# Fourier mixing beside attention: sequence matrices first, by two levels of seven products

## The chip, the cores and the metric

The kernel runs on one core of a Trainium2 chip. The metric is the device time of one execution in microseconds (us). TensorE (PE in the profile) multiplies matrices into PSUM; VectorE (DVE), ScalarE (ACT) and GpSimd (POOL) work elementwise; SyncE (SP) issues nearly all transfers. The kernel before takes 2942.41 us (median of three runs, 2941.58 to 2943.34).

## The reference

Two independent sublayers on a sequence of 2048 rows and 1024 features, in fp32, written side by side:

```python
qkv = (x @ wqkv)...; p = softmax(q @ k.T * 32 ** -0.5); a = (p @ v) @ wo    # 32 heads of 32
re = einsum("bsd,ed->bse", x, dft_hid_re); im = einsum("bsd,ed->bse", x, dft_hid_im)
b = einsum("ts,bse->bte", dft_seq_re, re) - einsum("ts,bse->bte", dft_seq_im, im)
return concatenate([a, b], axis=-1)
```

The change touches only the second one. Its result is y = Cr x Wr - Ci x Wi (with W transposed), where the sequence matrices C are 2048 x 2048 and the feature matrices W are 1024 x 1024. The product may be taken from either side: first x W and then C (x W), or first C x and then (C x) W.

## The kernel before, in words

**Dense products.** Each fp32 operand is split into a high half (a rounded copy, "cast") and a low half (operand minus high half), and each product of 128x128 by 128x512 takes three matmuls: high·high, low·high, high·low (`group`, line 404 issues them). The operand that is loaded as weights is called a stationary piece (`piece`: 128 x 4 x 128, ring tiles `h` and `l`), the other one moving (`moving`: 128x512, tiles `slot`). `fetch` loads a term into `raw`, a second one into `g`, and adds or subtracts them (line 469); `halves` makes the high half on DVE (line 491), or on ACT where the flag `spare` is set (line 489), and the low half on POOL or DVE (line 494).

**Seven products.** Each large product is cut in halves in all three directions and done with seven half-size products instead of eight (Winograd's form; `ORDER` = 1, 2, 5, 6, 7, 3, 4). The factors are sums of quarters of the operands, made by `fetch`; the products are added into the four result quarters by `gather`, which reads PSUM on DVE (lines 950 to 967) and combines on POOL or DVE (lines 979 to 992). Sums needed twice are stored in DRAM (`s1_d`, `t1_d`, `s2_d`, `t2_d`).

**Fourier part.** `dense1` multiplies x (`in_xb`) with the two feature matrices (`in_wd`) by one level of seven, 8 row blocks by 2 matrices by 4 chunks by 3 matmuls for each of the seven, into `ab_d`. `dense2` then does the sequence matrices (`in_ct`, stationary) on `ab_d` (moving), again one level for each of the two matrices, 8 groups of 24 matmuls for each of 14 products, and adds the two results through `y_d`.

**Attention.** `qkv` makes queries, keys and values with the same dense scheme. For every head, `scores` computes 32 blocks of 128 x 1024 scores (line 1278), their maxima on DVE (line 1284) and exponentials with sums on ACT (line 1287). `transposed` computes the transposed scores in 64 blocks of 128x512 (line 1400), takes the exponential on ACT (line 1404), and multiplies with the values in three blocks per head, "P·V" (line 1419). `project` multiplies the heads' outputs with `wo`, 672 matmuls; its tiles take the room of attention's, so its loads wait for all heads (`behind`).

**The order of the work.** All engines' orders are written out ahead by a planner (class `Plan`, lines 57 to 245) that keeps a clock with fixed costs for each operation. Streams S (scores), T (transposed scores) and V (P·V) belong to attention; the dense matmuls stand in one list, `fills`, in the order qkv, dense1, dense2, project. The main loop at the end of the kernel function starts the next fill if no attention step is ready, or if

```python
nf / (FILL - RES) <= done / ATT
```

where nf counts fills started, done the TensorE cost of attention so far, RES is 400, and ATT the whole cost of attention. On the other engines the ready operation of lowest rank goes first: PSUM reads and maxima come ahead of casts, these ahead of sums. `choose` starts nothing on POOL while DVE runs an operation marked `two` (sums, low halves, casts), and nothing marked `two` on DVE while POOL runs. Rings of few buffers (6 `raw`, 3 `g`, 4 `h`, 4 `l`, 4 `e`) limit how far the vector work runs ahead of the matmuls.

Of the kernel before, what the change touches and what calls it, by code (L numbers as in the profile page):

```python
# [16 lines left out]
P = 128  # L17
# [203 lines left out]
def kernel(  # L221
# [26 lines left out]
    ab_d = [[[dram.tile([P, NB], F32, name=f"ab_d{m}_{e}_{k}") for k in range(NS)] for e in range(2)] for m in range(2)]  # L248

    s1_d = [[dram.tile([P, 4, P], F32, name=f"s1_d{x}_{i}") for i in range(8)] for x in (5, 6)]  # L250
    t1_d = [[dram.tile([P, NB], F32, name=f"t1_d{x}_{n}") for n in range(8)] for x in (5, 6)]
# [5 lines left out]
    u3_d = [[dram.tile([P, NB], F32, name=f"u3_d{i}_{m}") for m in range(2)] for i in range(8)]  # L257
    s2_d = [[[dram.tile([P, 4, P], F32, name=f"s2_d{x}_{i}_{k}") for k in range(4)] for i in range(8)] for x in (5, 6)]
    t2_d = [[[dram.tile([P, NB], F32, name=f"t2_d{x}_{m}_{k}") for k in range(8)] for m in range(2)] for x in (5, 6)]
    y_d = [[dram.tile([P, NB], F32, name=f"y_d{i}_{e}") for e in range(2)] for i in range(NS)]  # L260
# [101 lines left out]
    FILL = 3 * (7 * 24 * 4 + 7 * 16 * 4 + 7 * 8 * 16 + 2 * 8 * 4)  # L362
# [251 lines left out]
    def qkv():  # L614
# [216 lines left out]
        def qk_group(x, W, b, n, order=None):  # L831
# [3 lines left out]
            if p == 1 and n == 0:  # L835
                if early:
                    X[2 * b], X[2 * b + 1] = acc(b)
                else:
# [3 lines left out]
                  gather(p, 2 * b + n, qk_result(b + 8 * h[0], 2 * h[1] + n, early) if h else None, early, None if b % 2 else SCALE), order)  # L842

# [7 lines left out]
        for x, (p, blocks, v) in enumerate(STEPS[:10]):  # L851
            spare[0] = x < 5
# [77 lines left out]

    def gather(what, X, Y, u3, to, wrote, part=None, split=False):

# [13 lines left out]
        def finish(ps, last):  # L946
# [63 lines left out]
            if what in (2, 3):  # L1010
                return put(X.at, [X.users], X.last, ALU.add, to, wrote, part)
            if Y is None:
                return put(lambda: got["c"], [cusers], cload, ALU.subtract, to, wrote, part)
            return put(Y.at, [Y.users], Y.last, ALU.subtract, to, wrote, part)
# [3 lines left out]
    ab_st = [[[[] for _ in range(NS)] for _ in range(2)] for _ in range(2)]  # L1018

    def dense1():  # L1020
        s1, t1 = ({5: [[] for _ in range(8)], 6: [[] for _ in range(8)]} for _ in range(2))
        u3 = [[[], []] for _ in range(8)]

        def a_terms(p, i):
            q = lambda r, k: xb[8 * r + i, :, 4 * k : 4 * k + 4, :]
            return {
                1: [(1, q(0, 0), [])], 2: [(1, q(0, 1), [])], 4: [(1, q(1, 1), [])],
# [17 lines left out]
        def load_b(x, n):  # L1045
            p = ORDER[x]
            B[x][n] = moving((8 * x + n) % 12, b_terms(p, n), (t1_d[p - 5][n], t1[p][n]) if p in (5, 6) else None)

# [542 lines left out]
```

## Time and profile before

| what | value |
|---|---|
| median of three runs | 2942.41 us |
| span of the profiled execution | 2940.5 us |
| matmuls in it | 14920, of them 6720 fills, 8 to warm up, 4096 for scores, 4096 P·V |
| DMA | 562.78 MB, mean 191 GB/s |
| dense1 | loads of its operands from 605.0 us, last store of its result 1460.4 us |
| dense2 | loads of the sequence matrices from 1371.2 to 2753.3 us |
| last P·V block ends | about 2760.5 us |

The profiled execution is one of its own; the time of a run contains some 2 us outside the span from the first to the last instruction. In tables of stretches each row gives start, end and length, then for each engine the busy us and the instructions in brackets, the granted clock as a share, the DMA engines' busy share and GB/s. In groups by line, the numbers behind the first bar are busy us in total and mean ns of one operation, and behind the second the idle time just before them with what ended it. In the order of time, each row has start, length, engine, line and operation, and in square brackets idle time before it.

### The profile page before, as it was taken

What the parts mean: (1) busy time and instruction counts of PE and PEld (TensorE: products, weight loads), DVE (VectorE), ACT (ScalarE), POOL (GpSimd) and SP (SyncE); (2) the same over time, 40 slices, a digit from 0 to 9 for tenths busy, and PEclk for the clock granted to TensorE, in tenths of its full rate; (3) what the DMA queues carried; (4) which work ended last, traced back from release to release, by engine and by line L of the source; (5) the groups of instructions that cost most, each with busy time, mean ns of one, the idle gap of its engine ahead of it and who ended that gap; (6) DMA issues with size and microseconds to landing.
All of it is one profiled execution on the core that took longest, in us unless ns stands there. A gap on an engine that the chain in (4) does not pass through costs nothing.

```text
span 2940.5 us, 45511 instructions
## 1 busy us (share of the span) xinstructions
PE 2934.3 (100%) x14920; PEld 2146.0 (73%) x14920; DVE 2328.2 (79%) x3196; ACT 2278.3 (77%) x4317; POOL 833.3 (28%) x650
## 2 busy tenths in 40 slices
PE   9999999999999999999999999999999999999999
PEld 8887777777777767777777777777777777677787
DVE  7679888788877987777777898888777888887585
ACT  5347888888888888888888888888888888887431
POOL 2324335132212332241111332333112333343042
PEclk9999999999999999999999999999999999999999
DMA  9965668676525653664425775554334677555663
GB/s 372 348 229 194 195 191 292 194 251 225 191 93 164 226 189 111 205 206 147 150 84 161 237 224 189 171 167 151 110 110 139 220 238 222 168 178 176 211 209 118
DMA packets 378455, 562.78 MB, mean 191 GB/s; under 512 B 111183, under 2 KB 111439, under 8 KB 378095
## 3 DMA queue, kind: packets, MB, share of 16 engines
q1 hardware_dynamic: 378076, 559.75, 58.8%
q8 instruction: 120, 1.97, 0.3%
q14 instruction: 115, 0.93, 0.1%
q10 hardware_dynamic: 144, 0.13, 0.0%
HBM read 385.65 MB, written 174.08 MB: 190 GB/s over the span
## 4 chain that ended last, share of the span: by engine, by line
PE 98%; DMA 1%; DVE 1%; ACT 0%; issue 0%; POOL 0%; SPq 0%; DVEq 0%; POOLq 0%; ACTq 0%
PE pd L404 44%; PE psT L1400 16%; PE psS L1278 16%; PE pd L1419 15%; PE psT L404 7%; DVE negm L1284 0%; DMA raw<-in_xb 0%; DMA g<-in_ct 0%; DMA raw<-ab_d 0%; ACT psS L1287 0%; DMA g<-in_xb 0%; DMA slot<-in_xw 0%; DVE l L494 0%; POOL raw L469 0%; DVE raw L469 0%
## 5 line engine op out<-in xcount | busy, mean ns | idle before, releaser
L1404 ACT ACTIVATE pt<-psT 128x512 f32<-128x512 f32 x2048 | 1193.8, 671 | 347.3 <-PE psT L1400 345.5
L1284 DVE TENSOR_REDUCE negm<-psS 128x1 f32<-128x1024 f32 x1024 | 1241.2, 1220 | 211.5 <-PE psS L1278 204.4
L1287 ACT ACTIVATE psS<-psS,negm 128x1024 f32<-128x1024 f32 x1024 | 1188.9, 1161 | 70.9 <-DVE negm L1284 66.8
L404 PE MATMUL pd<-slot,h 128*128 128x512 f32 x3400 | 1155.7, 389 | 0.0
L1400 PE MATMUL psT<-qs,ks 128*128 128x512 f32 x2048 | 802.3, 395 | 0.0
L404 PEld LDWEIGHTS pd<-slot,h 128*128 128x128 f32 x3400 | 638.3, 188 | 132.6
L404 PE MATMUL pd<-slot,l 128*128 128x512 f32 x1700 | 661.3, 389 | 0.0
L1400 PEld LDWEIGHTS psT<-qs,ks 128*128 128x128 f32 x2048 | 381.4, 188 | 157.3 <-issue 63.7
L1278 PE MATMUL psS<-ks,qs 128*128 128x512 f32 x1552 | 472.1, 390 | 0.7 <-ACT psS L1287 0.6
L1419 PE MATMUL pd<-pt,vt 128*32 128x512 f32 x4096 | 459.3, 594 | 0.0
L494 POOL TENSOR_TENSOR l<-raw,h 128x512 fp32r<-128x512 f32 x143 | 184.7, 1292 | 707.8 <-PE psT L1400 366.5
L404 PEld LDWEIGHTS pd<-slot,l 128*128 128x128 f32 x1700 | 319.1, 188 | 67.3 <-issue 0.8
L494 POOL TENSOR_TENSOR slot<-raw,slot 128x512 fp32r<-128x512 f32 x162 | 208.4, 1291 | 535.5 <-DVE slot L491 197.6
L469 POOL TENSOR_TENSOR raw<-raw,g 128x512 f32<-128x512 f32 x186 | 241.9, 1306 | 397.4 <-DMA raw<-t_d 48.9
L1278 PEld LDWEIGHTS psS<-ks,qs 128*128 128x128 f32 x1552 | 290.7, 188 | 62.2 <-ACT psS L1287 3.3
L1419 PEld LDWEIGHTS pd<-pt,vt 128*32 128x32 f32 x4096 | 123.3, 110 | 282.6 <-issue 265.7
L1287 ACT ACTIVATION_READ_ACCUMULATOR psS<-psS,negm 128x1 f32 x1024 | 285.9, 279 | 0.0
L404 PE MATMUL pd<-slot,slot 128*128 128x512 f32 x768 | 191.9, 389 | 0.0
L1432 DVE TENSOR_TENSOR ot<-ot,pd 128x512 f32<-128x512 f32 x64 | 44.0, 687 | 155.1 <-PE pd L1419 154.9
L404 PEld LDWEIGHTS pd<-slot,slot 128*128 128x128 f32 x768 | 144.2, 188 | 30.0
L491 DVE CAST h<-raw 128x512 fp32r<-128x512 f32 x321 | 147.5, 461 | 17.4 <-PE pd L404 14.2
L1278 PE MATMUL psS<-ks,qx 128*128 128x512 f32 x496 | 149.1, 391 | 0.0
(130 smaller groups left out, 1858.4 us busy)
## 6 DMA issues: line engine op xcount, KB each, us to landing
raw<-in_ct SPq DMA_DIRECT2D x192, 256.0 KB
qk_d<-e SPq DMA_DIRECT2D x52, 512.0 KB
qs<-qk_d SPq DMA_DIRECT2D x128, 192.0 KB
ks<-qk_d SPq DMA_DIRECT2D x128, 192.0 KB
raw<-ab_d SPq DMA_DIRECT2D x96, 256.0 KB
g<-in_ct SPq DMA_DIRECT2D x96, 256.0 KB
c<-u_d SPq DMA_DIRECT2D x88, 256.0 KB
s_d<-raw SPq DMA_DIRECT2D x80, 256.0 KB
```

The source lines that it names most:

```text
L404: nc.tensor.matmul(box["ps"], a[1]((a[0].hi, a[0].lo)[u]()), b[1]((b[0].hi, b[0].lo)[v]()), start=k == 0, stop=k == n - 1)
L469: (nc.gpsimd if e == "POOL" else nc.vector).tensor_tensor(out=dest(), in0=dest() if a is None else a.get(), in1=other["q"] if "q" in other ...
L491: nc.vector.tensor_copy(hi(), raw())
L494: (nc.gpsimd if e == "POOL" else nc.vector).tensor_tensor(out=lo(), in0=raw(), in1=f(hi()), op=ALU.subtract)
L1278: nc.tensor.matmul(p[:, i * NB : i * NB + NB], (QX[0] if own else QS[h % 2])[:, qt * P : qt * P + P], KS[h % 2][:, c * 1024 + i * NB : c * ...
L1284: nc.vector.tensor_reduce(out=ST["negm"][:, c, qt : qt + 1], in_=box["p"], axis=AX.X, op=ALU.max, negate=True)
L1287: nc.scalar.activation(box["p"], box["p"], AF.Exp, bias=ST["negm"][:, c, qt : qt + 1], accum_out=ST["sums"][:, c, qt : qt + 1])
L1400: nc.tensor.matmul(box["p"], KS[h % 2][:, t * P : t * P + P], QS[h % 2][:, j * NB : j * NB + NB], start=True, stop=True)
L1404: nc.scalar.activation(box["t"], box["p"], AF.Exp)
L1419: nc.tensor.matmul(po["p"][j * DH : j * DH + DH, :], VT[h][:, k, :], box["t"], start=(k == t0), stop=(k == t), tile_position=(0, j * DH),)
L1432: nc.vector.tensor_tensor(out=po["o"], in0=po["o"], in1=po["p"], op=ALU.add)
```

## The change

`dense1` now multiplies the sequence matrices first, and with two levels of seven: each of the two matrices (r = 0 cosine, r = 1 sine) takes 49 products (pp outer, p inner), each of 2 groups of 12 matmuls. x is stationary (`xb`), the sequence matrix moves (`ct`). A quarter of it, or a sum of two quarters, is held in 16 resident tiles `R` in fp32 for one outer product; the inner products' moving operands are made from `R` in place. The stationary pieces are stored when r = 0 makes them (`ha_d`) and loaded back for r = 1 (`again`). `gather2` adds the inner products in PSUM reads and two accumulators, then the outer ones through `xo_d` and `yo_d`, into `g_d`. `dense2` then does the feature matrices with one level of seven, both matrices in one sum, so `y_d` and its sums go.

`aside`, called in the steps 5 to 7 of `qkv` once after each group, makes the first 30 entries of the list `todo_a` ahead: the 28 stationary pieces of the outer products 1 and 2 and two sums of outer product 5. `spare` stays set after the early steps, so ACT may take casts in all of the Fourier part and of `qkv`. FILL follows the new count of matmuls. Nothing is changed in attention and projection.

```diff
-    FILL = 3 * (7 * 24 * 4 + 7 * 16 * 4 + 7 * 8 * 16 + 2 * 8 * 4)
+    FILL = 3 * (7 * 24 * 4 + 2 * 49 * 2 * 4 + 7 * 8 * 8 + 2 * 8 * 4)
...
+            if 5 <= x < 8:
+                aside((12, 13, 14))
...
         for x, (p, blocks, v) in enumerate(STEPS[:10]):
-            spare[0] = x < 5
+            spare[0] = True
...
+        def outer(y, e, users):
+            if pp == 1:
+                x_at[1][:] = [store(x_at[0], y, e, users)]
+            elif pp == 5:
+                y_at[1][:] = [store(y_at[0], y, e, users)]
+                o = combine(cx[0], cx[0], y, ALU.add, [e, cx[2]], [users, cx[1]])
+                x_at[1][:] = [store(x_at[0], cx[0], o, cx[1])]
+            elif pp == 4:
+                o = combine(y, cy[0], y, ALU.subtract, [e, cy[2]], [users, cy[1]])
+                wrote.append(store(to, y, o, users))
+            else:
+                o = combine(y, cx[0], y, ALU.add, [e, cx[2]], [users, cx[1]])
...
+    def a_piece(pp, p, i):
+        s = lambda x: (si_d[0][pp][x - 5][i], si.setdefault((pp, x, i), []))
+        terms = a_terms(pp, p, i)
+        a = piece(terms, s(p) if p in (5, 6) else None)
+        rank = seq()
+        kept_a[pp, p, i] = [op("SP", ISSUE, lambda k=k, t=t: nc.sync.dma_start(ha_d[pp][p][i][:, k * NB : k * NB + NB], ...), [made], [u], rank, 256)
+                            for k, (t, made, u) in enumerate(zip((a.hi, a.lo), a.made, a.users.lists))]
+        return a
...
+        def b_outer(r, pp, k, n, kk):
+            terms = {
+                1: [(1, *q(0, 0))], 2: [(1, *q(1, 0))], 3: [(1, *q(1, 1))],
+                5: [(1, *q(0, 1)), (-1, *q(0, 0))], 6: [(1, *q(1, 1)), (-1, *t(5))],
+                7: [(1, *q(1, 1)), (-1, *q(0, 1))], 4: [(1, *t(6)), (-1, *q(1, 0))],
+            }[pp]
+            fetch([P, NB], terms, t(pp) if pp in (5, 6) else None, R[j])
...
+        def load_b(x, kk):
+            terms, keep = {
+                1: ([(1, r(0, 0))], None), 2: ([(1, r(1, 0))], None), 3: ([(1, r(1, 1))], None),
+                5: ([(1, r(0, 1)), (-1, r(0, 0))], r(0, 0)), 6: ([(1, r(1, 1)), (-1, r(0, 0))], r(0, 0)),
+                7: ([(1, r(1, 1)), (-1, r(0, 1))], r(0, 1)), 4: ([(1, r(0, 0)), (-1, r(1, 0))], r(1, 0)),
+            }[p]
+            M[x, kk] = moving((4 * x + kk) % 10, terms, None, keep)
...
+        for x, (r, pp, p) in enumerate(steps):
...
+            for i in range(2):
+                a = again(pp, p, i) if (pp, p, i) in kept_a else a_piece(pp, p, i)
...
+                group(((chunk(a, c), (M[x, c], whole)) for c in range(4)), 4,
+                      gather2(pp, p, X[i], Y[i] if p not in (1, 2) else None, (xo_d[r][pos], xo[r][pos]), (yo_d[r][pos], yo[r][pos]), to, wrote))
```

353 lines of the change are left out of this document (249 added, 104 removed).

## The prediction

> **What bounds the kernel now.** I read the page's first two parts first, then the same stretches for all engines and for single lines, and last the instructions in order of time around one P·V block.
>
> ```profile
> span 2940.5 us, 45511 instructions
> PE 2934.3 (100%) x14920; PEld 2146.0 (73%) x14920; DVE 2328.2 (79%) x3196; ACT 2278.3 (77%) x4317; POOL 833.3 (28%) x650
> ...
> PE   9999999999999999999999999999999999999999
> ```
>
> TensorE is never idle, so taking matmuls away looks worth their time. The stretches show why that reading is too short. All engines first; the cuts lie where attention starts (200), where the matmuls of qkv end (772) and where attention ends (2762):
>
> ```profile
> 200.00:772.00 572.00, 572.00 (x2937) 415.25 (x2936) 480.48 (x658) 478.53 (x911) 195.71 (x153) 1.00 0.68 219
> 772.00:1376.00 604.00, 603.66 (x3137) 431.93 (x3139) 476.16 (x635) 515.17 (x985) 152.51 (x119) 1.00 0.53 168
> 1376.00:2000.00 624.00, 623.77 (x3237) 448.57 (x3230) 504.66 (x687) 531.83 (x1019) 163.01 (x127) 1.00 0.55 172
> 2000.00:2600.00 600.00, 599.88 (x3120) 428.82 (x3119) 486.38 (x660) 510.54 (x979) 167.27 (x130) 1.00 0.54 168
> ```
>
> Now the dense matmuls alone (line 404, the "fills"):
>
> ```profile
> 0.00:200.00 200.00, 190.53 (x831) 155.82 (x831) 1.00 0.91 333
> 200.00:772.00 572.00, 340.94 (x1183) 221.81 (x1182) 1.00 0.68 219
> 772.00:1376.00 604.00, 348.09 (x1187) 222.73 (x1187) 1.00 0.53 168
> 1376.00:2000.00 624.00, 357.22 (x1227) 230.44 (x1228) 1.00 0.55 172
> 2762.00:2940.50 178.50, 174.63 (x771) 144.25 (x769) 1.00 0.55 195
> ```
>
> and the transposed scores of attention (line 1400):
>
> ```profile
> 200.00:772.00 572.00, 168.64 (x432) 80.38 (x432) 1.00 0.68 219
> 772.00:1376.00 604.00, 190.58 (x487) 90.42 (x486) 1.00 0.53 168
> 1376.00:2000.00 624.00, 199.25 (x508) 94.72 (x508) 1.00 0.55 172
> 2000.00:2600.00 600.00, 189.69 (x484) 90.15 (x484) 1.00 0.54 168
> ```
>
> Attention moves at one steady pace, 0.81 of these scores per us, whichever Fourier stage lies beside it. The fills take what is left: 1187 in 604 us, 1.96 per us. The order of the program says the same: a fill goes ahead of attention that is ready only where nf / (FILL - RES) <= done / ATT. FILL - RES is 6240 - 400 = 5840. At 1376 us 831 + 1183 + 1187 = 3201 fills are gone, 0.55 of it, and of attention 432 (200 to 772) + 487 of 2048 transposed scores, 0.45. So fills are ahead and attention has the right of way. What sets attention's pace is ScalarE, 511 of 600 us busy, and the rest is mostly one kind of gap:
>
> ```profile
> L1404 ACT ACTIVATE pt<-psT 128x512 f32<-128x512 f32 x2048 | 1193.8, 671 | 347.3 <-PE psT L1400 345.5
> ```
>
> and in order of time:
>
> ```profile
> 1001.39 4.50 PE L1419 MATMUL pd<-pt,vt 128*32 128x512 f32 x40
> ...
> 1006.35 0.60 ACT L1404 ACTIVATE pt<-psT 128x512 f32<-128x512 f32 x1 [2.33 <-PE psT L1400]
> ```
>
> For the 4.50 us of a P·V block TensorE makes no scores and ScalarE runs dry for 2.33 us. There are three such blocks in each of 32 heads, and fills are in none of them. **So there are two bounds at once: TensorE as a sum, and the chain of attention through ScalarE, which ends at 2762 us and which fewer fills don't shorten.** Behind it 771 fills stand, 672 of them the output projection (7·8·4·3), so only 99 are Fourier fills that come late.
>
> **The change part by part.** Every operation is on a 128x512 tile; the counts are read off the loops.
>
> Matmuls. Before: feature stage 7·8·2·12 = 1344, sequence stage 14·8·24 = 2688. After: sequence matrices 2·49·2·12 = 2352, feature matrices 7·8·24 = 1344. That is 336 fewer.
>
> ```profile
> 2800.00:2900.00 100.00, 100.00 (x443) 82.79 (x442) 1.00 0.52 175
> ```
>
> A fill costs 100/443 = 0.2257 us, so 75.8 us of TensorE go.
>
> Vector work. "Two-input" are sums and low halves, for POOL or DVE; casts are high halves; "out" reads PSUM and is DVE's.
>
> - Before, both stages: 768 two-input, 448 casts, 256 out, 1056 transfers.
> - After: sequence stage 1070 two-input (580 sums, 490 low halves), 490 casts, 224 out; feature stage 272, 168 and 64. Together 1342, 658, 288, and about 1654 transfers.
>
> The added work is 574 two-input operations and 210 casts, for fewer matmuls, and it is not spread evenly. The first matrix (cos) makes the stationary pieces, the second (sin) loads them back. 28 pieces, those of the first two of seven outer products, are made early by `aside`. So per fill: the first 336 fills about 0.34 two-input and 0.17 casts; the next 840 (outer products five to four of the first matrix) 482/840 = 0.57 and 210/840 = 0.25; the 1176 of the second matrix 442/1176 = 0.38 and 0.17. Today's sequence stage has 0.21 and 0.125. Out is 0.095 throughout. The prices:
>
> ```profile
> L1284 DVE TENSOR_REDUCE negm<-psS 128x1 f32<-128x1024 f32 x1024 | 1241.2, 1220 | 211.5 <-PE psS L1278 204.4
> L491 DVE CAST h<-raw 128x512 fp32r<-128x512 f32 x321 | 147.5, 461 | 17.4 <-PE pd L404 14.2
> L494 DVE TENSOR_TENSOR l<-raw,h 128x512 fp32r<-128x512 f32 x178 | 127.5, 717 | 3.5
> L494 POOL TENSOR_TENSOR l<-raw,h 128x512 fp32r<-128x512 f32 x143 | 184.7, 1292 | 707.8 <-PE psT L1400 366.5
> L967 DVE TENSOR_TENSOR e<-slot,pd 128x512 f32<-128x512 f32 x126 | 85.9, 682 | 40.9 <-PE pd L404 38.1 <-issue 0.8
> L489 ACT ACTIVATE slot<-raw 128x512 fp32r<-128x512 f32 x58 | 35.6, 630 | 82.6 <-PE psT L404 34.8 <-DVE raw L469 15.6 <-DMA raw<-in_wo 15.4
> ```
>
> The plan (`choose`) starts no POOL operation while DVE is in a two-input operation or a cast, and the reverse; maxima and PSUM reads may lie beside POOL. Attention takes 1024 maxima in some 2500 us, 0.41 per us, at 1.22 = 0.50 of DVE, and its small operations about 0.055 (estimate from their groups). In the heavy stretch at r fills per us, with casts on ScalarE in its gaps (0.15 per us; gaps of 347 us in 2500 would hold 0.22), the best split is r = 1.48: two-input 0.85 per us, of which DVE 0.34 · 0.717 = 0.25 and POOL 0.51 · 1.292 = 0.65; casts on DVE 0.22 · 0.461 = 0.10; out 0.14 · 0.682 = 0.10. DVE is then 0.50 + 0.055 + 0.25 + 0.10 + 0.10 = 1.00, and DVE's share of the port plus POOL 0.25 + 0.10 + 0.65 = 1.00. Nothing is left, and the fills want 1.96. No stretch so far shows such packing; the highest is
>
> ```profile
> 200.00:300.00 100.00, 100.00 (x481) 76.74 (x480) 90.14 (x120) 75.91 (x141) 43.24 (x34) 1.00 0.60 188
> 400.00:500.00 100.00, 100.00 (x509) 73.56 (x501) 87.97 (x125) 87.02 (x168) 54.82 (x44) 1.00 0.78 254
> ```
>
> so I take r = 1.40; bounds 1.2 (DVE at 85%) and 1.5. The second matrix needs by the same sum at 1.96 about 0.95 of DVE; I take 1.96, bound 1.8.
>
> ```profile
> 1001.19 1.28 POOL L469 TENSOR_TENSOR raw<-raw,g 128x512 f32<-128x512 f32 x1 [8.56 <-issue]
> ...
> 1001.50 1.22 DVE L1284 TENSOR_REDUCE negm<-psS 128x1 f32<-128x1024 f32 x1 [0.33 <-PE psS L1278]
> ```
>
> Beside a maximum a POOL sum is no longer than alone. The Trainium skill ("SBUF — State Buffer", Who interferes with whom) states this exclusion for the hardware: a DVE operation with two SBUF inputs, or a cast in a two-port mode, and a GpSimd operation that reads SBUF block each other, a reduction does not. These rows agree for the reduction; that the other two block each other no row here can show, as the plan never lets them meet. Were there no exclusion, POOL could run through, the heavy stretch would keep 1.96, and the sum would be that of the first rival.
>
> Transfers, all on SP's queue:
>
> ```profile
> qs<-qk_d SPq DMA_DIRECT2D x128, 192.0 KB
> ks<-qk_d SPq DMA_DIRECT2D x128, 192.0 KB
> ...
> L453 SPq DMA_DIRECT2D raw<-in_ct x192: 327/333/1007, 1371.2 to 2753.3; - x192
> ```
>
> The second sweep has 532 in 1176 fills, 0.45 · 0.262 MB · 1.96 = 232 GB/s, and attention's own about 32 (estimate: these two and five smaller kinds, 2.5 MB per head of 79 us): 264. The issues take 0.9 per us at 0.33, a third of SP. The row 400:500 above carries 254 at 0.78 with TensorE full. I cost it at nothing; without that cover, 5% off the pace of this sweep is 30 us there and 13 at the end.
>
> ScalarE's casts. `spare` is now true behind the early steps too, so ScalarE may take casts inside attention. In a P·V gap they are free, but the last one overruns it: 96 gaps by half of 0.63 is 30 us at most. DVE's queue delays maxima by up to 0.72 us, which two score buffers mostly hide. I put attention's end 25 us later, bounds 0 and 80.
>
> The sum. Fill 2016 ends at 772 as now (`aside` in 200 to 400 costed at nothing, covered by fills that are far ahead). 336/1.96 = 171, to 943; 840/1.40 = 600, to 1543; 1176/1.96 = 600, to 2143. Attention ends at 2762 + 25 = 2787; by then 644 · 1.96 = 1262 of the feature stage's 1344 fills are gone and 82 are left: 82/4.43 = 18.5. Projection 672/4.43 = 152, then 4.5 as now (178.5 less 771/4.43). End 2787 + 18.5 + 152 + 4.5 = 2962. The median of the three runs, 2942.4, lies 1.9 above the profiled span, so **2964**. Seen as TensorE's sum: 75.8 us are saved and some 97 come back as idle time, nearly all in the heavy stretch and where attention is stretched.
>
> **Rivals.**
>
> - *The fills keep up, attention sets the end.* Condition: the heavy stretch runs at 1.5 or above and attention is not delayed. Then nothing of the feature stage is left behind 2762, the projection starts after its loads:
>
> ```profile
> 2762.04 0.32 SPq L1450 DMA_DIRECT2D o_d<-ot  x1
> ...
> 2769.05 1.33 ACT L489 ACTIVATE slot<-raw 128x512 fp32r<-128x512 f32 x2 [14.78 <-DMA raw<-in_wo]
> ```
>
>   the store of the last head at 2762.04, its first cast at 2769.05, a first product about 2771.5 (estimate), and the end is 2771.5 + 152 + 4.5 = 2928, as a time 2930: faster by 0.4%. For it: POOL is idle 72% today. Against: the sum above at 1.00 of both engines. 0.17.
> - *TensorE alone is the bound*, attention speeds up as fills go: 2942.4 - 75.8 = 2867. Against: the pace of 0.81 and the gaps, which no fill lies in. 0.03.
> - *Halfway:* r near 1.45, attention delayed by 10: the same sum gives 2946. 0.15.
> - *Attention itself is slowed,* by casts on ScalarE and maxima behind sums: 80 us late, r = 1.2 (700 us) leaves 170 fills at 2842, 38 us: 3038. 0.10.
> - *Transfers limit the second sweep too*: 2964 + 13 = 2977. 0.05.
>
> **Numbers.** My forecast, 2950 to 2990, has 0.50. A measurement tells 0.2%, some 6 us, from no change. Faster 0.17 + 0.03 = 0.20; within 0.15; slower 0.50 + 0.10 + 0.05 = 0.65. The range goes from the first rival's 2930, less 4 for an earlier attention, to 3020; outside are the full gain and most of the slowed attention, with tails some 0.15.
>
> **What would show it.** Right: TensorE idle for the first time between about 940 and 1540, fills near 1.4 per us there, DVE over 90% and POOL over 55%; the transposed scores still near 0.8 per us; a last P·V block at 2762 or later. The step on attention fails if that block ends well before 2750; the step on vector work fails if TensorE stays full through the first matrix. If TensorE idles just ahead of the projection instead, the first rival is right. If the idle time lies elsewhere, behind waits for transfers, I have mistaken the engine.

## The result and the profile after

The changed kernel takes 2982.18 us (median of four runs, 2977.93 to 2986.48) against 2942.19 for the one before on the same chip (2941.58 to 2943.34). The ratio is 1.0135, with a 95% interval of 1.0121 to 1.015: slower by 1.35%, 18 us above the forecast and inside its range. The profiled execution took 2978.95 us; its span is 2977.2 us, 36.7 more than before.

First the head of the page:

```profile
span 2977.2 us, 47160 instructions
PE 2909.6 (98%) x14584; PEld 2070.5 (70%) x14584; DVE 2438.9 (82%) x3296; ACT 2406.8 (81%) x4559; POOL 1429.0 (48%) x1124
...
q1 hardware_dynamic: 493084, 731.75, 74.8%
```

The 336 matmuls are gone (14920 to 14584), POOL has 474 operations more, and the queue of SP carries 731.75 MB; all of the core's transfers went from 562.78 MB to 734.89. The page alone would still let one think that TensorE is the bound, at 98%.

The stretches, all engines; the cuts are now where the matmuls of qkv end (797), where the first 336 fills of the sequence stage are done (974), the next 840 (1574), the 1176 of the second matrix (2184), and where attention ends (2797). Columns as before: start, end, length, busy us with instructions in brackets for PE, PEld, DVE, ACT, POOL, then granted clock, DMA share, GB/s:

```profile
200.00:797.00 597.00, 583.58 (x2959) 417.37 (x2957) 485.88 (x647) 512.30 (x977) 235.44 (x183) 1.00 0.80 263
797.00:974.00 177.00, 175.82 (x920) 123.81 (x920) 154.30 (x221) 157.14 (x304) 108.02 (x86) 1.00 0.78 252
974.00:1574.00 600.00, 557.16 (x2739) 355.54 (x2738) 528.47 (x689) 546.95 (x1044) 412.28 (x326) 1.00 0.88 290
1574.00:2184.00 610.00, 605.54 (x3136) 429.86 (x3135) 534.40 (x727) 546.59 (x1046) 406.83 (x322) 1.00 0.80 256
2184.00:2797.00 613.00, 612.39 (x3196) 434.74 (x3195) 466.16 (x637) 508.67 (x971) 160.44 (x125) 1.00 0.54 167
2797.00:2977.20 180.20, 176.57 (x778) 145.83 (x778) 126.53 (x180) 49.69 (x83) 56.20 (x43) 1.00 0.55 190
```

The fills alone (line 404 is now 406), first columns PE and PEld:

```profile
797.00:974.00 177.00, 98.30 (x336) 63.13 (x337) 1.00 0.78 252
974.00:1574.00 600.00, 254.73 (x842) 157.47 (x843) 1.00 0.88 290
1574.00:2184.00 610.00, 343.70 (x1178) 220.56 (x1176) 1.00 0.80 256
2184.00:2797.00 613.00, 361.55 (x1238) 232.09 (x1238) 1.00 0.54 167
2797.00:2977.20 180.20, 176.57 (x778) 145.83 (x778) 1.00 0.55 190
```

In the third stretch of the first table the fills fall from 1.96 to 842/600 = 1.40 per us and are back at 1.93 in the next. At 1.96 there would have been 1176 in 600 us; the missing 334 at 0.2257 us are 75.4 us of TensorE, as much as the change saves in all (75.8). The busy column hides it: 557 of 600 us look like 43 us of idle time, because a matmul that stands alone is booked at some 0.39 us though a row of them takes 0.2257 each. Rates have to be counted in instructions. The Trainium skill ("Perfetto Trace Analysis", Identifying the Most-Contended Engine) says that TensorE's matmul busy share is no good measure of how close a kernel is to its limit. This trace agrees, with 43 us against 75.

The transposed scores (line 1400 is now 1620) tell of attention:

```profile
974.00:1574.00 600.00, 195.09 (x483) 89.84 (x483) 1.00 0.88 290
1574.00:2184.00 610.00, 189.70 (x483) 90.08 (x483) 1.00 0.80 256
2184.00:2797.00 613.00, 197.80 (x504) 93.88 (x504) 1.00 0.54 167
```

They run at 0.80 per us beside the starved fills as beside the others; before it was 0.81. Freed TensorE time did not make attention faster. What stood ahead of the exponentials of these scores changed instead (groups by line, idle time behind the second bar):

```profile
L1624 ACT ACTIVATE pt<-psT 128x512 f32<-128x512 f32 x2048 | 1195.6, 672 | 247.1 <-PE psT L1620 244.5
```

ScalarE's gaps in front of these exponentials shrank from 347.3 to 247.1 us in all. Casts now lie in them:

```profile
246.00:2790.00 2544.00, 140.57 (x212) 1.00 0.76 245
```

That is line 491 on ACT from 246 us to 2790 us: 212 casts, 140.57 us, where there were none between 243 and 2762 us before. (Five more stand on line 1189.) The gaps took up 100 of the 140.57 us at most, and attention ends at 2797.0 us instead of 2760.5.

Last, what holds the fills. In the third stretch the sums, casts and low halves (lines 471, 493 and 496; DVE's and POOL's share of each, casts are DVE's alone):

```profile
974.00:1574.00 600.00, 85.64 (x119) 100.78 (x79) 1.00 0.88 290
974.00:1574.00 600.00, 72.15 (x128) 1.00 0.88 290
974.00:1574.00 600.00, 14.96 (x22) 241.53 (x190) 1.00 0.88 290
974.00:1574.00 600.00, 4.88 (x7) 65.24 (x50) 1.00 0.88 290
```

The fourth row is line 1050, the combining in two accumulators. DVE's four entries, 177.6 us, and all of POOL's 412.3 may not overlap by the rule in `choose`. Together they are 589.9 of 600 us, 0.98. That is the row-by-row form of the prediction's "nothing is left", and it shows the wall better than DVE's 88% or POOL's 69%. The planner's clock is not the chip's, though: laid over each other, the records of the two overlap for 45 us of the 600, so that at least one of the two engines is inside such an operation for 0.90 of the stretch. Experiment 8 shows that in an overlap DVE mostly waits. The same sum over the stretch 772 to 1376 of the kernel before is some 0.41, without the combining.

### The profile page after: what moved, and what is told of

Its sections match the earlier page's. It is cut to its first block, busy times and chain, and to the rows that moved or that the text cites. A ratio compares the mean times of both kernels' runs of the same rounds, so it can differ in the third digit from the quotient of the medians.

```text
span 2977.2 us, 47160 instructions
## 1 busy us (share of the span) xinstructions
PE 2909.6 (98%) x14584; PEld 2070.5 (70%) x14584; DVE 2438.9 (82%) x3296; ACT 2406.8 (81%) x4559; POOL 1429.0 (48%) x1124
## 2 busy tenths in 40 slices
DMA packets 493477, 734.89 MB, mean 247 GB/s; under 512 B 121230, under 2 KB 154254, under 8 KB 493102
## 3 DMA queue, kind: packets, MB, share of 16 engines
q1 hardware_dynamic: 493084, 731.75, 74.8%
q8 instruction: 118, 1.93, 0.3%
## 4 chain that ended last, share of the span: by engine, by line
PE 79%; ACT 7%; DMA 7%; DVE 4%; issue 2%; POOL 1%; SPq 1%; DVEq 0%; POOLq 0%; ACTq 0%
PE pd L406 35%; PE pd L1639 13%; PE psT L1620 12%; PE psS L1498 12%; PE psT L406 6%; ACT psS L1507 5%; ACT pt L1624 3%; DVE negm L1504 2%; DMA slot<-in_ct 1%; DMA m_d<-lt 1%; DMA qs<-m_d 1%; DMA ha_d<-slot 0%; DMA g<-in_ct 0%; DMA c<-xo_d 0%; DVE slot L493 0%
## 5 line engine op out<-in xcount | busy, mean ns | idle before, releaser
L1624 ACT ACTIVATE pt<-psT 128x512 f32<-128x512 f32 x2048 | 1195.6, 672 | 247.1 <-PE psT L1620 244.5
L1507 ACT ACTIVATE psS<-psS,negm 128x1024 f32<-128x1024 f32 x1024 | 1195.5, 1168 | 51.1 <-DVE negm L1504 49.4
L406 PE MATMUL pd<-slot,h 128*128 128x512 f32 x3176 | 1081.4, 390 | 1.6 <-POOL slot L496 0.8
L406 PEld LDWEIGHTS pd<-slot,h 128*128 128x128 f32 x3176 | 596.2, 188 | 128.3 <-DVE h L493 1.5
L406 PE MATMUL pd<-slot,l 128*128 128x512 f32 x1588 | 619.6, 390 | 8.6 <-POOL l L496 8.4
L496 POOL TENSOR_TENSOR slot<-slot,slot 128x512 fp32r<-128x512 f32 x312 | 399.2, 1292 | 262.0 <-PE psS L1498 45.9
L1498 PE MATMUL psS<-ks,qs 128*128 128x512 f32 x1552 | 479.9, 395 | 29.8 <-ACT psS L1507 28.6
L406 PEld LDWEIGHTS pd<-slot,l 128*128 128x128 f32 x1588 | 298.1, 188 | 74.8 <-POOL l L496 13.5
L496 POOL TENSOR_TENSOR l<-raw,h 128x512 fp32r<-128x512 f32 x126 | 162.5, 1290 | 294.4 <-PE psT L1620 83.2
L496 POOL TENSOR_TENSOR slot<-raw,slot 128x512 fp32r<-128x512 f32 x95 | 122.9, 1298 | 265.9 <-ACT slot L491 92.4
L471 POOL TENSOR_TENSOR raw<-raw,g 128x512 f32<-128x512 f32 x106 | 137.8, 1304 | 171.3 <-DVE ot L1668 17.1
L471 POOL TENSOR_TENSOR slot<-slot,slot 128x512 f32<-128x512 f32 x103 | 131.9, 1292 | 37.2 <-DVE slot L493 17.7
```

The source lines that it names most:

```text
L406: nc.tensor.matmul(box["ps"], a[1]((a[0].hi, a[0].lo)[u]()), b[1]((b[0].hi, b[0].lo)[v]()), start=k == 0, stop=k == n - 1)
L471: (nc.gpsimd if e == "POOL" else nc.vector).tensor_tensor(out=dest(), in0=dest() if a is None else a.get(), in1=other["q"] if "q" in other ...
L496: (nc.gpsimd if e == "POOL" else nc.vector).tensor_tensor(out=lo(), in0=raw(), in1=f(hi()), op=ALU.subtract)
L1498: nc.tensor.matmul(p[:, i * NB : i * NB + NB], (QX[0] if own else QS[h % 2])[:, qt * P : qt * P + P], KS[h % 2][:, c * 1024 + i * NB : c * ...
L1507: nc.scalar.activation(box["p"], box["p"], AF.Exp, bias=ST["negm"][:, c, qt : qt + 1], accum_out=ST["sums"][:, c, qt : qt + 1])
L1624: nc.scalar.activation(box["t"], box["p"], AF.Exp)
```

## The experiments

**1. The kernel before with 336 fills fewer.** Are there two bounds, or is TensorE's sum alone the bound?

```diff
-                        for k in range(0, 8, 4):
+                        for k in range(0, 4 if i > 5 else 8, 4):
```

> The kernel before with 336 dense matmuls left out of its sequence stage and nothing added: in 28 of its 112 groups (the last two row blocks of each product) only the first four of eight chunks are multiplied, and the pieces for the others are not made. So it has the matmul count of the changed kernel and less vector work than either. Theory: attention through ScalarE sets the end; its last P·V block still ends at 2755 to 2765 us, nothing of the Fourier part is left behind it, and the time is 2928 to 2935. Rival: TensorE's sum is the bound; the time is 2942 - 75.8 = 2866.

Measured: 2932.52 us, ratio 0.9967 (0.9955 to 0.9978). Up to about 2659 us the fills stand as close as before, so attention is the same there (487 transposed scores between 772 and 1376 us in both kernels). Only behind that point has TensorE nothing but attention to do. The transposed scores there, in the kernel before and in this one:

```profile
2660.00:2750.00 90.00, 32.85 (x85) 15.72 (x85) 1.00 0.49 157
...
2660.00:2750.00 90.00, 49.32 (x89) 19.64 (x89) 0.81 0.03 10
```

There are 85 scores beside 207 fills, 89 beside none, and the last exponential ends at 2750.7 us instead of 2754.3. Attention makes little use of a free TensorE, and the 75.8 us bring 10. Part of that may be the granted clock, 0.81 in this stretch (see the last section). What they leave shows in the end of the span, all engines:

```profile
2700.00:2720.00 20.00, 18.21 (x64) 6.11 (x63) 0.69 (x1) 12.63 (x23) 0.00 (x0) 0.80 0.02 5
2720.00:2740.00 20.00, 19.00 (x61) 6.38 (x61) 0.69 (x1) 11.84 (x21) 0.00 (x0) 0.67 0.00 0
...
2760.00:2780.00 20.00, 11.77 (x31) 8.36 (x32) 10.88 (x16) 8.17 (x13) 1.28 (x1) 0.57 1.01 351
2780.00:2800.00 20.00, 17.46 (x73) 14.10 (x72) 16.09 (x24) 8.76 (x15) 7.78 (x6) 0.94 1.01 356
```

The fills run out at about 2659 us, some 62 matmuls stand in 20 us instead of 104, and the projection can start only when the last head is stored and its weights are loaded (DMA share 1.01). TensorE as the only bound falls. What 336 fewer fills bring with no price, and with attention as it is, is 0.3%: the change had 10 us to win.

**2. The first sweep with fewer transfers.** Vector work or transfers?

```diff
-        kept_a[pp, p, i] = [op("SP", ISSUE, ...
...
+            terms = terms[:1] + [(sign, R[j]) for sign, *_ in terms[1:]]
...
-                a = again(pp, p, i) if (pp, p, i) in kept_a else a_piece(pp, p, i)
+                a = again(pp if pp < 3 else 1, p, i) if r or pp < 3 else a_piece(pp, p, i)
```

> The changed kernel with transfers taken away and all vector work kept: the second term of a resident tile's sum is the tile itself instead of a loaded quarter (same operation, 128 loads of 256 KB fewer), and the stationary pieces of outer products 5, 6, 7, 3, 4 are not stored (140 stores fewer); the second matrix loads those of products 1 and 2 in their place, as many transfers as before. In the heavy stretch (840 fills, 974 to 1574 us) nearly 30% of the bytes go. Theory: DVE and POOL under their exclusion set the pace; the stretch stays at 570 to 610 us (1.38 to 1.47 fills per us) and the time at 2965 to 2985. Rival: transfers (0.9 of the DMA engines busy there) or their latency set it; the fills go to 1.8 per us or more, the stretch takes under 470 us and the time falls to 2940 to 2955.

Measured: 2978.3 us, ratio 1.0122 (1.0107 to 1.0137). The heavy stretch, all engines:

```profile
964.00:1542.00 578.00, 544.06 (x2704) 350.04 (x2703) 505.40 (x679) 529.65 (x1016) 398.56 (x322) 0.99 0.67 209
```

The DMA share falls from 0.88 to 0.67 and the stretch only from 600 to 578 us; stretch and time are as expected. Transfers are at most 22 of the 600 us and not what holds the stretch.

**3. No low halves of the moving pieces in the Fourier stage's first product.** Vector work taken away, transfers kept.

```diff
+        if only:
+            a = op("DVE", CAST, ...)
+            return Piece(h, h, (a, a), mine)
```

> The changed kernel with vector work taken away and all transfers and matmuls kept: in the sequence stage the moving operand's low half is not made (392 two-input operations fewer, 140 of the 482 in the heavy stretch); the third matmul of each product takes the high half again. Theory: two-input work per fill goes from 0.57 to 0.41, the same split of engines gives 1.78 fills per us instead of 1.40, the heavy stretch takes 460 to 490 us instead of 600, the fills are done before attention ends, and the time is 2945 to 2958. Rival, transfers set the pace: the stretch stays at 570 to 610 us and the time at 2970 to 2985.

Measured: 2995.05 us, ratio 1.0182 (1.0167 to 1.0197). The heavy stretch:

```profile
962.00:1475.00 513.00, 489.42 (x2453) 326.68 (x2453) 445.31 (x621) 454.97 (x868) 300.35 (x237) 0.99 0.98 332
```

Shorter by 87 us, so vector work was the wall, but 513 us is more than the 460 to 490 expected: the DMA engines are now at 0.98. And the time rose: attention ends at 2817, 20 us later than in the change itself. The expected time was missed.

**5. Both of them** in one kernel, told here because it answers 3.

```diff
+            terms = terms[:1] + [(sign, R[j]) for sign, *_ in terms[1:]]
...
+                a = again(pp if pp < 3 else 1, p, i) if r or pp < 3 else a_piece(pp, p, i)
...
+            M[x, kk] = moving((4 * x + kk) % 10, terms, None, keep, True)
```

> Both omissions together: no low halves of the moving operand in the sequence stage, and of the transfers the second terms of the resident sums and the storing of pieces are left out. Theory: with the vector work gone it was the full DMA queue (0.97 to 1.00 busy from 900 to 1400) that delayed attention's own transfers there and so its end (2816); with fewer bytes the heavy stretch takes 430 to 480 us, the 1024th transposed score is done by 1520 to 1528 instead of 1541, attention ends at 2775 to 2795, and the time is 2948 to 2970. Rival: casts on ScalarE and queued maxima delay attention whatever the DMA does; attention ends at 2805 or later and the time stays at 2985 to 2998.

Measured: 2960.93 us, ratio 1.0062 (1.0042 to 1.0082).

```profile
963.00:1437.00 474.00, 463.19 (x2362) 320.27 (x2361) 405.98 (x571) 430.95 (x826) 305.12 (x249) 0.99 0.78 248
```

474 us, 1.77 fills per us, DMA at 0.78, and attention ends at 2786, 31 us ahead of 3. Stretch, end and time are as expected. Against 2 only the low halves are gone, and the stretch falls from 578 to 474 us: with transfers out of the way, vector work is what holds it. Against 3 the vector work is the same and only transfers differ: there the DMA engines were full, and attention was late. Which of attention's waits the transfers made longer was not followed. In the change the heavy stretch stands at 0.88, so transfers are the next limit right behind the vector work.

**4. No casts on ScalarE inside attention.**

```diff
-            spare[0] = True
+            spare[0] = x < 5
...
-                      [made], [users], 10 + rank, other=("ACT", ACAST, 25 + rank), two=True)
+                      [made], [users], 10 + rank, other=("ACT", ACAST, 25 + rank) if spare[0] else None, two=True)
```

> The changed kernel with the flag spare as before (ScalarE takes casts only in the early steps and in the projection); all else as changed. Theory: ScalarE is relieved, so attention ends 10 to 25 us earlier (2772 to 2787 instead of 2797), but DVE takes some 0.12 casts per us more, the heavy stretch goes from 600 to 640 to 670 us, and the time is 2985 to 3010. Rival, the casts on ScalarE delay attention and that is what costs: attention ends at 2765, the heavy stretch keeps 600 us, and the time falls to 2955 to 2965.

Measured: 3032.02 us, ratio 1.03 (1.0282 to 1.0317).

```profile
1005.00:1650.00 645.00, 602.80 (x2913) 377.45 (x2913) 566.60 (x791) 551.92 (x1054) 434.72 (x344) 0.98 0.84 272
```

The heavy stretch takes 645 us, as expected. Between the 512th and the 1024th transposed score attention lost less than 1 us against before, where the change loses 10: without casts on ScalarE this delay is gone, though the fills are also sparser there. But attention ends at 2841 instead of earlier, because the fills are so late (4368 of them at 2280 us; 2184 in the change) that the rule nf / (FILL - RES) <= done / ATT comes to hold and puts fills ahead of attention. Counted from the trace's matmuls with the planner's own costs, its two sides are 0.699 and 0.695 at 2000 us, 0.733 and 0.733 at 2100, and 0.951 and 0.951 at 2700; in the change they are 0.765 and 0.733 at 2100. ScalarE's gaps in front of the exponentials grow to 385.8 us, though no cast lies in them (347.3 before): the scores come later. That the rule is what delays attention is worked out from these counts and wasn't tried by itself. The expected end and time were missed: I had looked at ScalarE and not at the rule of the order.

**6. No `aside`.**

```diff
-            if 5 <= x < 8:
-                aside((12, 13, 14))
```

> The changed kernel without the 30 entries made ahead in qkv; all pieces are made in the first sweep. Theory: qkv's fills end at 773 to 780 as before the change (797 with it), the 256th transposed score is back at 552 to 556 (564), the first 336 fills take 200 to 230 us instead of 177, the heavy stretch stays near 600; attention ends at 2780 to 2790 and the time is 2965 to 2980. Rival, the work made ahead is nearly free in qkv and dear in the first sweep: the first 336 fills take over 240 us and the time is above 2985.

Measured: 2975.49 us, ratio 1.0116 (1.01 to 1.0131). The qkv fills end at 778 us instead of 797; the next 336 take 213 us instead of 177, the heavy ones 592. Attention ends at 2795, 5 us above the expected 2780 to 2790; the time is as expected. The price of `aside` is real but its work must be done somewhere, and comes back behind 778 us: against the kernel before, attention is only 5 us late at the 256th transposed score, but 32 us at the 1536th, and ends 2 us earlier than in the change. The spreads of the two kernels' times overlap (2974.38 to 2981.24 and 2977.93 to 2986.48 us).

**7. The kernel before with casts on ScalarE allowed throughout.**

```diff
-            spare[0] = x < 5
+            spare[0] = True
```

> The kernel before with the flag spare set as in the changed one, nothing else: ScalarE may take casts all through attention. Theory: a hundred or two of casts go to ScalarE, each P·V gap ends with an overrun, and attention ends 8 to 20 us later; time 2950 to 2962. Rival, the gaps swallow them: attention ends within 4 us of 2760 and the time is 2940 to 2945.

Measured: 2964.94 us, ratio 1.0074 (1.0057 to 1.0091). Line 489 on ACT:

```profile
243.00:2754.00 2511.00, 72.26 (x108) 1.00 0.57 182
```

108 casts of 0.67 us, and attention ends at 2787.7 us instead of 2760.5: 0.25 us per cast. Delay and time lie above the 8 to 20 us and the 2950 to 2962 that I expected. The gaps in front of the exponentials:

```profile
L1404 ACT ACTIVATE pt<-psT 128x512 f32<-128x512 f32 x2048 | 1191.5, 669 | 302.9 <-PE psT L1400 300.8 <-PE pd L1419 0.8
```

They gave up 44.4 us (347.3 before), the casts take 72.3, and the 28 us left over are nearly the delay of 27. That the gaps behind P·V swallow the casts falls.

**8. The change without the exclusion of DVE and POOL in the order.** Does the exclusion lie in the order alone or in the chip?

```diff
-        if e == "POOL" and self.ported[0] > self.now - self.BEHIND:
+        if False:
...
-        if e == "POOL" or e == "DVE" and o.two:
-            self.port = self.free[e]
```

> The changed kernel with the plan's rule taken out that keeps POOL and DVE's two-input operations and casts apart (and the wait that goes with it). Theory, the two engines exclude each other in the hardware: the mean two-input operation of DVE goes from 0.70 to 0.75 us to over 0.9, POOL's from 1.29 to 1.4 or more, the heavy stretch stays at 560 to 660 us, and the time is 2965 to 3020. Rival, only the plan keeps them apart: durations stay, the heavy stretch falls under 500 us until the DMA engines are full, and the time is 2950 to 2995 with fills done ahead of attention.

Measured: 3253.99 us, ratio 1.106 (1.1043 to 1.1076). Groups by line, of this kernel (its lines are two below those of the change):

```profile
L494 POOL TENSOR_TENSOR slot<-slot,slot 128x512 fp32r<-128x512 f32 x291 | 424.2, 1465 | 258.0 <-DVE slot L491 220.5 <-ACT slot L489 28.2 <-PE psT L1618 4.0
L491 DVE CAST slot<-slot 128x512 fp32r<-128x512 f32 x331 | 230.1, 711 | 2.1 <-PE pd L404 1.7 <-DMA slot<-in_ct 0.3
L469 DVE TENSOR_TENSOR slot<-slot,slot 128x512 f32<-128x512 f32 x124 | 137.8, 1126 | 3.1 <-POOL slot L469 2.4 <-POOL slot L494 0.2
L1505 ACT ACTIVATE psS<-psS,negm 128x1024 f32<-128x1024 f32 x1024 | 1141.5, 1115 | 327.4 <-DVE negm L1502 323.9 <-DVE tt L1566 1.6 <-DVE nm L1525 0.4
```

and the same groups of the change:

```profile
L496 POOL TENSOR_TENSOR slot<-slot,slot 128x512 fp32r<-128x512 f32 x312 | 399.2, 1292 | 262.0 <-PE psS L1498 45.9 <-DVE slot L471 39.1 <-DVE slot L493 35.3
L493 DVE CAST slot<-slot 128x512 fp32r<-128x512 f32 x264 | 135.2, 536 | 3.7 <-PE pd L406 1.9 <-DMA slot<-in_ct 1.5
L471 DVE TENSOR_TENSOR slot<-slot,slot 128x512 f32<-128x512 f32 x121 | 82.2, 710 | 0.1
L1507 ACT ACTIVATE psS<-psS,negm 128x1024 f32<-128x1024 f32 x1024 | 1195.5, 1168 | 51.1 <-DVE negm L1504 49.4
```

A sum on DVE goes from 710 to 1126 ns, a cast from 536 to 711, a low half on POOL from 1292 to 1465: the chip excludes, not only the written order. These means mix operations that meet and others that don't. Sorted by whether DVE's operation begins inside one of POOL's, the records of this kernel give 684 ns for a sum that meets none (93 of them) and 1335 for one that begins inside (179), and 418 and 917 ns for casts. The maximum, a reduction, takes 1218 and 1214 ns.

The trace of the kernel before could have told the same, because there the two do meet now and then:

```profile
2814.27 1.30 POOL L494 TENSOR_TENSOR slot<-raw,slot 128x512 fp32r<-128x512 f32 x1 [1.29 <-DVE s L469]
...
2814.88 1.24 DVE L469 TENSOR_TENSOR s<-a,s 128x512 f32<-128x512 f32 x1
```

The sum begins 0.61 us into POOL's operation and ends 0.55 us behind its end, after 1.24 us instead of 0.68. In that kernel 58 sums on DVE begin inside an operation of POOL's and take 973 ns in the mean, 142 meet none and take 684. The heavy stretch takes 617 us, no shorter than with order. The time is far above the expected 2965 to 3020: ScalarE waits 323.9 us for maxima instead of 49.4. A maximum is no longer than before, so it starts later; that it stands behind a blocked DVE operation is my reading of this. The Trainium skill ("SBUF — State Buffer", Who interferes with whom) has the engine that comes second blocked for the whole instruction of the first; these times, each between one operation and the sum of two, agree.

**9, 10, 11. Four P·V blocks per head instead of three**, in the kernel of experiment 1, in the change, and in the kernel before: shorter gaps of ScalarE, so the chain of attention itself is made shorter.

```diff
-ENDS = (0, 5, 10, 16)
+ENDS = (0, 4, 8, 12, 16)
```

> The kernel before with the same 336 matmuls left out as in the first experiment, and P·V in four blocks of four score rows per head instead of three of five, five and six. TensorE has some 66 us to spare there, and each block starves ScalarE less. Theory, the gaps of ScalarE at P·V set attention's pace: attention ends 15 to 45 us before 2760, and the time is 2890 to 2920 (2932.5 with three blocks). Rival, something else paces attention: its end stays within 5 us and the time is 2928 to 2945.

> The changed kernel with P·V in four blocks of four per head. Theory: attention ends 15 to 40 us before 2797, more Fourier fills are left behind it, each at 0.23 us instead of 0.51, and TensorE pays 13 us for 32 more blocks; time 2955 to 2972. Rival, in the changed kernel the vector work paces everything: attention's end moves by less than 8 us and the time is 2978 to 3000.

> The kernel before with P·V in four blocks of four per head, for comparison. Theory: TensorE's sum binds as well there, so an earlier end of attention (15 to 40 us) only leaves more fills behind it and 13 us of block overhead are added; time 2940 to 2960. Rival, attention alone binds: 2905 to 2930.

Measured: 2920.62 us, ratio 0.9928 (0.9913 to 0.9943), attention's end 2744.5; 2987.49, 1.0155 (1.014 to 1.0171), end 2807; 2957.76, 1.0052 (1.0035 to 1.0068), end 2776. The gaps, in 1 and in 9:

```profile
L1404 ACT ACTIVATE pt<-psT 128x512 f32<-128x512 f32 x2048 | 1196.7, 671 | 335.1 <-PE psT L1400 329.3
L1404 ACT ACTIVATE pt<-psT 128x512 f32<-128x512 f32 x2048 | 1182.2, 653 | 303.5 <-PE psT L1400 299.9
```

335.1 us became 303.5, attention ends 12 us earlier than there (2756.9) and 16 us earlier than in the kernel before, and the time falls by 12 us, to just above the 2890 to 2920 that I expected: TensorE has room.

In the kernel before the same edit costs 16 us. The time is as expected; the way to it is not, since attention ends 16 us later instead of earlier. TensorE's busy time grows by 13.0 us (2934.3 to 2947.3), the price of 32 more blocks. Attention is 5 us earlier up to the 1536th transposed score and loses 22 us behind it. There the rule of the order, counted as in 4, has come to hold: 0.911 and 0.911 at 2500 us, against 0.926 and 0.901 in the kernel before. So the fills, later by the blocks' price, take the right of way from attention. That fits TensorE's sum as the second bound; taking the rule out was not tried. A shorter chain helps only with fewer fills, so both bounds hold in the kernel before at once.

In 10 the edit was expected to help and does not (attention ends 10 us later, time inside the rival's range). ScalarE's gaps shrink there too (247.1 to 229.4 us), but attention is 15 us late against the change by the 1536th transposed score. This is nearer to the rival, the vector work setting the pace, which is not shown by it.

**12. The change without `aside` and with casts on ScalarE in `dense1` only.**

```diff
-            if 5 <= x < 8:
-                aside((12, 13, 14))
...
-            spare[0] = True
+            spare[0] = x < 5
...
+        spare[0] = False
```

> The changed kernel without the pieces made ahead, and with casts on ScalarE allowed only in the sequence stage. Theory: attention is delayed only there, so its end comes at 2780 to 2788 instead of 2797; the fills are no later than without the work ahead (5712th at 2823) by more than 10 us; time 2962 to 2974, the best of the change but still above the kernel before. Rival: without ScalarE's casts in qkv and in the feature stage the fills fall behind as in the run without any, and the time is 2980 to 3010.

Measured: 2995.5 us, ratio 1.0183 (1.0168 to 1.0198); heavy stretch 597 us, second sweep 624, attention's end 2802. Missed by some 20 us upward and inside the rival's range: taking away two things that had each looked like a cost (6 and 7) made the kernel slower. Attention is level with the kernel before up to the 512th transposed score (869 us) and 37 us late at the 1536th (2174). Why this second sweep is slower than that of the change (610 us) stays open.

No version that computes everything beat the kernel before.

## Why the prediction was right, step by step

| step | predicted | measured |
|---|---|---|
| fills run dry in the first sweep, rate | 1.40 per us, 943 to 1543 | 1.40, 974 to 1574 |
| first 336 fills | 171 us | 177 |
| second sweep | 600 us | 610 |
| `aside` | nothing | qkv's fills end 24 us late |
| attention's end | 2762 + 25 = 2787 | 2797 |
| fills left behind attention, without the projection | 82 | 106 |
| span | 2962 | 2977.2 |

**Two bounds.** Right, and shown by 1: 336 fewer fills alone end at 2932.5, so the first rival's 2930 was the floor of any such change that leaves attention as it is. Experiment 9 shows the chain as a bound by shortening it (2920.6); 11 fits TensorE's sum as the other.

**The heavy stretch.** Right in place, length and cause. The price list and the exclusion gave 1.48 as the best packing and 1.40 with the discount; 842 fills in 600 us are 1.40. That it came out to two digits is partly luck: 1.40 was picked between bounds of 1.2 and 1.5, and the same sum at 1.40 puts DVE at some 0.98 and POOL at 0.61, where 0.88 and 0.69 were measured. So the split between the two engines was off, and the sign "DVE over 90%" did not come true. That vector work is the wall is shown (2 leaves the stretch as it is, 3 and 5 shorten it). That it is the turns of DVE and POOL rests on their sum of 0.98, on the blocked operations and on 8, which shows that dropping the turns from the order doesn't get around them. Whether more buffers in the rings would have packed the two closer was not tried.

Two smaller parts failed. The prediction says that no row can show the two engines blocking each other, as the plan never lets them meet; in the trace before they do meet, 58 times with a sum alone (experiment 8). And I held transfers clear of this stretch by working them out for the second sweep (264 GB/s, measured 256), while the heavier one is the first, which stores its pieces as well: 290 GB/s at 0.88. By experiment 2 that cost at most 22 us of the stretch and hardly anything of the time (2978.3 us); experiment 3 ran into it.

**`aside` at nothing.** Failed. "Covered by fills that are far ahead" was the step. Its work lies where qkv's own vector work and transfers are already dense, all engines, after and before:

```profile
300.00:400.00 100.00, 95.37 (x475) 67.26 (x473) 86.03 (x120) 86.59 (x167) 53.55 (x42) 1.00 0.96 328
```

```profile
300.00:400.00 100.00, 100.00 (x531) 71.15 (x529) 77.92 (x109) 85.53 (x165) 31.77 (x26) 1.00 0.58 180
```

DMA goes from 0.58 to 0.96 and TensorE loses 56 instructions in 100 us, 8 of them fills and 48 attention's. So the lead of the fills does not cover the work, since attention is delayed as well: the exponential of the 256th transposed score, at 552 us before, ends at 564 us. Whether transfers or vector work do it was not separated. Experiment 6 gives most of it back: the fills of qkv end at 778 us and the 256th exponential at 557. The sign "TensorE idle for the first time between about 940 and 1540" failed with `aside` too: TensorE is already idle for 13 us between 200 and 797.

**Attention's end.** Right in sign, mis-sized: 25 predicted, 35 measured by the cuts. The lateness at the exponential of the 256th, 512th, 1024th, 1536th and 2048th transposed score is 12, 16, 26, 28 and 37 us: a third arises in the stretch of `aside`, 10 us in the heavy stretch, 8 in the feature stage. My mechanism was casts that are longer than the gap they start in, priced at 30 us at most. Experiment 7 shows that casts on ScalarE delay attention, at 0.25 us for each of 108. It is not a fixed price, as 212 casts in the change would then be 53 us. The sum of casts less what the gaps gave up fits in 7 (28 us for 27) and roughly in the change (140.6 - 100.2 = 40 for 37), but not in 6 (51 for 35). How the 37 us divide between casts, full transfers and the order is not settled: 4, 6 and 12 each took one or two of these away, and attention ended at 2841, 2795 and 2802. Above all, 6 took the first third away and the end hardly moved. So it is in part luck that the forecast of this end came within 10 us. Each edit also changes the written order of all engines; how much of such differences is due to that alone was not tried.

**The end.** 15 us of difference in the span are 10 from attention's end and 5 from 106 instead of 82 fills behind it (24/4.43). In the kernel before it was 99. So the tail is as it was (178.5 and 180.2 us), and the whole loss of 36.7 us is attention that ends later; the saved TensorE time was spent in the heavy stretch before it could shorten anything.

**The rivals.** The first (fills keep up) needed 1.5 fills per us and got 1.40; TensorE alone was refuted by 1; halfway, attention delayed by 10, had the delay too small; the slowed attention had the right direction, but 35 us were measured of its 80, and 1.40 fills per us where it had 1.2; transfers in the second sweep: it ran at 0.80 of the DMA engines and 1.93 fills per us and took 610 us, 10 of the rival's 30 us at most.

## What to carry to other kernels

Price a saving in one engine's sum against every chain that does not contain it, and find the floor first: here the saving at no price at all would have bought 0.3%. Where two engines take turns at one resource, add their exclusive times over the stretch that is heaviest, not over the kernel; that sum, 0.98, showed the wall while each engine alone looked looser (0.88 and 0.69). A written order that keeps two engines apart holds only as far as its clock matches the chip's, so look for overlaps in the trace. Moving work to an engine that paces the kernel, or into a stretch whose transfers are dense already, isn't free just because that engine has idle time or because its stream is ahead. And a rule that shares one engine by progress, as this planner's does, gives the right of way to whoever is late.

## What the runs showed of the hardware

- **The granted clock of TensorE halves when it is only partly used, in steps of 3.41 us.** The 0.80, 0.67 and 0.57 of experiment 1 are mixtures. Cut where the clock record changes, the same end of the span reads (all engines):

```profile
2720.00:2732.00 12.00, 12.00 (x28) 4.13 (x32) 0.00 (x0) 7.76 (x13) 0.00 (x0) 0.50 0.00 0
2733.00:2739.00 6.00, 5.16 (x31) 1.59 (x19) 0.69 (x1) 3.16 (x6) 0.00 (x0) 1.00 0.00 0
2740.00:2753.00 13.00, 12.03 (x30) 4.64 (x34) 0.00 (x0) 8.18 (x15) 0.00 (x0) 0.50 0.00 0
2760.50:2776.50 16.00, 8.27 (x17) 5.56 (x18) 9.59 (x14) 8.17 (x13) 1.28 (x1) 0.50 1.00 346
2777.50:2797.00 19.50, 17.87 (x79) 14.45 (x77) 14.38 (x21) 8.13 (x14) 7.78 (x6) 1.00 1.02 366
```

  The Trainium skill ("TensorE: Matmul & The Clock Gate", Part 1) knows a half and a full clock for a core that runs alone, switched in windows of some 3.4 us. The traces agree: the clock records of all 14 kernels hold 0.5 and 1.0 alone, each between two changes for a whole number of 3.413 us. How sparse the stream must be can be counted in the 12 traces with changes. Windows at the full clock with fewer than five matmuls were always followed by the half clock (38 of 38), those with five or six in 51 of 92 cases, those with seven or more in 7 of 10216; a row of fills without gaps holds 15 (3.41 / 0.2257). The heavy stretch of the change, with 2739 in 600 us (some 16 in 3.41), kept 1.00. A kernel that runs TensorE dry ahead of its last stage starts that stage slow: the first row of the projection above, from 2760.5 us, is at 0.50.
- **DVE and POOL block each other.** A sum of 128x512 on DVE that begins inside an operation of POOL's takes 1335 ns in the mean in experiment 8 and 973 in the kernel before, against 684 for one that meets none; it ends some 0.55 us behind the end of POOL's. A maximum takes 1.22 us beside POOL as without it.
- **Full DMA engines** (0.98 over 513 us in experiment 3) went with an attention that ended 31 us later than with 0.78 in experiment 5 at the same vector work.
